# A transformer block on one Trainium2 core: fewer wait instructions, and a semaphore of its own for the gate matmuls

## The chip, the cores and the metric

The kernel runs on one core of a Trainium2 chip. A core has TensorE (PE in the profile: matmuls; PEld: the weight loads that go with them), VectorE (DVE), ScalarE (ACT), GpSimd (POOL) and SyncE (SP), which issues most DMAs here. The engines run side by side, each in its own order, and wait for each other through semaphores. The metric is the device time of one execution in microseconds; lower is better.

## The reference

```python
def _A_ref(x, wqkv, wo):                      # x: 1 x 2048 x 448, 16 heads of 28
    qkv = (x @ wqkv) split in q, k, v by head
    phi = lambda t: jnp.where(t > 0, t + 1, jnp.exp(t)) + 1e-6
    pq, pk = phi(q), phi(k)
    kv = jnp.einsum("bhsd,bhse->bhde", pk, v)
    z = jnp.einsum("bhsd->bhd", pk)
    num = jnp.einsum("bhqd,bhde->bhqe", pq, kv)
    den = jnp.einsum("bhqd,bhd->bhq", pq, z)[..., None] + 1e-6
    return (num / den, heads joined) @ wo

def _B_ref(x, w_gate, w_up, w_down):          # 448 -> 1792 -> 448
    g = jnp.einsum("bsd,df->bsf", x, w_gate)
    u = jnp.einsum("bsd,df->bsf", x, w_up)
    return jnp.einsum("bsf,fd->bsd", _gelu(g) * u, w_down)

h = x + _A_ref(_layernorm(x), wqkv, wo)
h2 = h + _B_ref(_layernorm(h), w_gate, w_up, w_down)
```

All inputs are bf16. A layer norm and linear attention are followed by a second layer norm and a gated GELU network; both have a residual.

## The kernel before

The 2048 rows are cut into 16 tiles of 128. Stage A normalizes each tile (VectorE statistics, L359 and L360; ScalarE for the reciprocal root, L366 and L368; the normalizing itself on VectorE for tiles 0 to 3, L381, and on GpSimd for the rest, L399), transposes it (tiles 0 to 3 on TensorE, L389, the rest by DMA transposes on SyncE's queue, L401), makes q and k (L415), phi (L426 to L428), and adds up the product of k and the normalized rows (L434). From that come a small key-value matrix (L473) and a folded output matrix (L493). Then, in pairs of tiles (`a2_pair`), q is divided by its denominator: a product with `zbc` (L515, L531, mostly on GpSimd), a sum (L518, L532), a reciprocal, a product (L522, L536). It is transposed, multiplied with the folded matrix (L563, L573, L574), added to the residual (L579), normalized again (L591, L608), and transposed by DMA into `hnT` (L611; the first two tiles on TensorE).

Stage B works on chunks of 2, 2, 4, 4 and 4 tiles (`B1_CHUNKS`). For each, `gu_chunk` runs over the 1792 columns of the inner width, 128 at a time. One step of it, a gate/up task, is named `gu2_v` or `gu4_v`, with v from 0 to 55 in the order of the program text: 7 pairs of matmuls with 512 columns for four tiles, 14 pairs with 256 columns for two. A pair is a gate matmul on the upper 64 rows of the array (L672) and an up matmul on the lower 64 rows (L674), issued gate first; they can run at the same time. Gate and up results have two PSUM banks each, taken in turn, so task v+2 needs the banks of task v. ScalarE makes the GELU of the gate bank in two halves of 256 columns (`ge0_v`, `ge1_v`, L692) into one of three `gl` buffers. VectorE multiplies each half with the up bank into `hh` (`hm0_v`, `hm1_v`, L694). The GELUs release the gate bank, the products the up bank. When all of `hh` for a pair of tiles is there, the down matmuls (`b2_pair`, L642; for the last two tiles `b2_tile`, L624) and the final residual additions (L648, L628) follow, and SyncE writes the result out.

Nothing is scheduled when the kernel is built. Each operation is a task with a number, and the lists in `ORDERS` fix each engine's order of tasks by number, written out by hand; parts of stage B and of stage A are interleaved in them.

Waits are made in `emit`. A task knows the tasks that it depends on (`deps`, with a place `dep_at` inside the task for those whose matmuls wait at different points, `mw=True`). Each engine has one semaphore that counts its finished tasks; each loading DMA has its own. For each dependency `emit` calls `wait_ge` unless this engine has itself waited for as much before (`waited`); what the engine knows only through another engine's waits isn't taken into account. Among the waits of one place that with the higher count goes first:

```python
for d in sorted(t.deps, key=lambda d: (t.dep_at[d.idx] if t.mw else 0, -d.ticket)):
    if waited.get(d.sem.num, 0) < d.ticket:
```

An instruction holds one wait. In the built program it is the first of a place that stays in the instruction; the others become separate wait instructions on the engine's sequencer, one or two waits each, ahead of it. In the profile they are the EVENT_SEMAPHORE records with line L164, and have no busy time. A matmul's wait shows at its weight load. A gate/up task adds one to TensorE's count with its last instruction, the last up matmul.

## Time and profile before

| | |
|---|---|
| median of 3 runs | 195.69 us (195.64 to 196.22) |
| the profiled execution | 195.62 us, of which 193.9 from its first to its last instruction |
| granted TensorE clock | 1.00 of full speed |

Busy microseconds of the engines by stretch of the span, with the number of instructions left out:

| stretch, us | what runs | TensorE | VectorE | ScalarE | GpSimd |
|---|---|---|---|---|---|
| 0 to 13 | loads, first tiles of stage A | 11.35 | 8.40 | 8.20 | 6.41 |
| 13 to 33 | q, k and their product | 20.00 | 18.63 | 12.29 | 10.70 |
| 33 to 53 | small matrices, first pairs of `a2_pair` | 18.43 | 18.95 | 16.32 | 6.67 |
| 53 to 87 | stage B for tiles 0 to 3, more of `a2_pair` | 33.83 | 30.39 | 12.12 | 16.00 |
| 87 to 120 | stage B for tiles 4 to 7, the last of `a2_pair` | 32.76 | 23.46 | 10.42 | 7.22 |
| 120 to 180 | stage B for tiles 8 to 15 | 59.81 | 27.56 | 16.46 | 5.26 |
| 180 to 193.9 | last down matmuls, output | 11.45 | 3.98 | 1.21 | 0.00 |

How to read the lines that follow below: in the timeline a row is the start in microseconds from the first instruction, the length, engine, line, operation, output and inputs, shapes, and a count of merged instructions; brackets hold the engine's idle time before it and what ended that. "64*128 64x512" is a matmul on 64 rows of the array and 128 columns of it, with 512 moving columns. A matmul's end is modelled, and neighbours overlap in the records, so TensorE counts as busy even where it stands for a moment; the distance between two starts tells more. The chain of waits lists start, length and what worked, followed back from the end; "issue" is time for which the profile shows no wait, ACTq is ScalarE's sequencer. The view of waits gives an engine, what it was about to do and what it waited for: total us, times, longest. The view of one line gives an instruction's count and its shortest, median and longest duration in ns.

### The profile page before, as it was taken

The page shows a single profiled execution, that of the slowest core. Times are in us where ns is not written, and L with a number is a line of the kernel's source. Part 1 is how long each engine was busy: PE and PEld are TensorE (multiplying, and loading weights), DVE is VectorE, ACT ScalarE, POOL GpSimd, SP SyncE. Part 2 cuts the span into 40 slices and gives each one's busy share as a digit, 9 for nine tenths or more (in the row PEclk, how much of TensorE's full clock was granted, in tenths as well). Part 3 has the DMA queues.
Part 4 walks back from the last instruction along what each step waited for, and adds up shares of the span by engine and source line. Part 5 has one row for each costly group of instructions (what it writes and reads, how often), then busy time and mean ns, then how long its engine had stood idle before and what let it go on. Part 6 is the DMA issues. An engine that isn't in the chain of part 4 may idle for free.

```text
span 193.9 us, 4577 instructions
## 1 busy us (share of the span) xinstructions
PE 187.6 (97%) x1813; PEld 109.6 (57%) x1813; DVE 131.4 (68%) x326; ACT 77.0 (40%) x220; POOL 52.3 (27%) x93
## 2 busy tenths in 40 slices
PE   7999999989999999999999999999999999999994
PEld 7545445445588768775544347756444454555643
DVE  2799987999999976998857773528435524515232
ACT  3798743878974212323224331321441424211200
POOL 8067740740228284040019400002800000000000
PEclk9999999999999999999999999999999999999999
DMA  5973558995295503761200391000092100000035
GB/s 193 374 196 64 104 110 184 218 218 110 72 266 150 95 3 49 98 116 29 47 3 0 76 138 28 0 3 25 1 142 49 51 0 0 3 0 0 3 132 178
DMA packets 34597, 17.12 MB, mean 88 GB/s; under 512 B 26832, under 2 KB 33168, under 8 KB 34576
## 3 DMA queue, kind: packets, MB, share of 16 engines
q1 hardware_dynamic: 34432, 16.72, 39.3%
q8 instruction: 14, 0.23, 0.5%
q10 hardware_dynamic: 144, 0.11, 0.3%
q14 instruction: 7, 0.06, 0.1%
HBM read 8.26 MB, written 1.84 MB: 52 GB/s over the span
## 4 chain that ended last, share of the span: by engine, by line
PE 83%; DVE 10%; ACT 3%; issue 2%; DMA 1%; ACTq 0%; DVEq 0%
PE ps L674 29%; PE ps L642 18%; PE ps L672 12%; PE ps L415 9%; PE ps L434 5%; PE ps L624 3%; PE ps L573 3%; DVE hh L694 2%; PE ps L574 2%; ACT gl L692 1%; DMA x_sb<-in_A_x_dram 1%; DVE den L518 1%; DVE pqn L522 1%; DVE st L359 1%; DVE eq L528 1%
## 5 line engine op out<-in xcount | busy, mean ns | idle before, releaser
L674 PE MATMUL ps<-hnT,wgu_sb 64*128 64x512 bf16 (+1 forms) x490 | 89.8, 334 | 0.4
L672 PE MATMUL ps<-hnT,wgu_sb 64*128 64x512 bf16 (+1 forms) x490 | 89.8, 333 | 0.0
L692 ACT ACTIVATE gl<-ps 128x256 bf16<-128x256 f32 x112 | 36.8, 382 | 85.6 <-PE ps L674 73.6
L694 DVE TENSOR_TENSOR hh<-ps,gl 128x256 bf16<-128x256 f32 x112 | 43.2, 417 | 40.5 <-ACT gl L692 40.3
L674 PEld LDWEIGHTS ps<-hnT,wgu_sb 64*128 64x128 bf16 x490 | 44.4, 94 | 31.0 <-DVE hh L694 6.9
L672 PEld LDWEIGHTS ps<-hnT,wgu_sb 64*128 64x128 bf16 x490 | 44.8, 94 | 6.5 <-DVE hnT L606 0.2
L642 PE MATMUL ps<-wd_sb,hh 64*128 64x448 bf16 x392 | 41.7, 349 | 0.2 <-DVE hh L694 0.2
L642 PEld LDWEIGHTS ps<-wd_sb,hh 64*128 64x128 bf16 x392 | 23.4, 94 | 14.9 <-DVE hh L694 1.6
L415 PE MATMUL ps<-wqk_sb,xnT 128*128 128x448 bf16 x128 | 27.4, 352 | 0.0
L359 DVE BATCH_NORM_STATS2 st<-x_sb 128x6 f32<-128x448 bf16 x32 | 19.1, 614 | 3.7 <-DMA x_sb<-in_A_x_dram 3.5
L415 PEld LDWEIGHTS ps<-wqk_sb,xnT 128*128 128x128 bf16 x128 | 12.1, 98 | 11.3 <-DVE pk L428 0.5
L531 POOL TENSOR_TENSOR t<-pq,zbc 128x448 f32<-128x448 bf16 x12 | 12.6, 1067 | 16.5 <-DVE pq L529 16.5
L434 PE MATMUL ps<-pk,xnn 128*128 128x448 bf16 x64 | 14.3, 353 | 0.0
L648 DVE TENSOR_TENSOR x_sb<-ps,x_sb 128x448 bf16<-128x448 f32 x14 | 8.4, 618 | 7.7 <-PE ps L642 7.7
L573 PE MATMUL ps<-w,pqnT 64*128 64x448 bf16 x49 | 11.5, 349 | 0.1
L363 POOL TENSOR_SCALAR nm<-mv 128x1 f32<-128x1 f32 (+1 forms) x19 | 4.1, 228 | 26.6 <-DVE mv L360 26.3
L426 ACT ACTIVATE e<-ps 128x448 bf16<-128x448 f32 x16 | 8.6, 540 | 5.6 <-PE ps L415 3.0
L399 POOL TENSOR_SCALAR xnn<-x_sb,nm,rs 128x448 bf16<-128x448 bf16 x12 | 9.6, 804 | 3.5 <-ACT rs L368 3.1
L608 POOL TENSOR_SCALAR hn<-x_sb,nm,rs 128x448 bf16<-128x448 bf16 x14 | 10.3, 745 | 0.5
L574 PE MATMUL ps<-pt_sb,pqnT 64*128 64x448 bf16 x42 | 10.2, 350 | 0.0
L371 POOL TENSOR_SCALAR ln<-mv 128x2 f32<-128x2 f32 x7 | 1.5, 222 | 32.1 <-DVE mv L360 31.9
L579 DVE TENSOR_TENSOR x_sb<-ps,x_sb 128x448 bf16<-128x448 f32 x16 | 9.7, 615 | 0.7 <-PE ps L574 0.6
(83 smaller groups left out, 166.9 us busy)
## 6 DMA issues: line engine op xcount, KB each, us to landing
out_dram<-x_sb SPq DMA_DIRECT2D x15, 112.0 KB, 1.8
wd_sb<-in_B_w_down_dram SPq DMA_DIRECT2D x1, 1568.0 KB, 7.5
x_sb<-in_A_x_dram SPq DMA_DIRECT2D x3, 448.0 KB, 5.6
wgu_sb<-in_B_w_gate_dram SPq DMA_DIRECT2D x1, 896.0 KB, 12.8
wgu_sb<-in_B_w_up_dram SPq DMA_DIRECT2D x1, 896.0 KB, 15.8
wqk_sb<-in_A_wqkv_dram SPq DMA_DIRECT2D x1, 672.0 KB, 4.5
wgu_sb<-in_B_w_gate_dram SPq DMA_DIRECT2D x1, 672.0 KB, 5.8
wgu_sb<-in_B_w_up_dram SPq DMA_DIRECT2D x1, 672.0 KB, 8.3
```

Source lines behind the costliest of these rows:

```text
L359: op("dve", lambda e: e.bn_stats(st[:, t, :], src_ap), [b_src], [b_st[t]], "bnst%s_%d" % (tag, t))
L415: ins = e.matmul(ps[:, bk, 0:D], xnT[:, t, k, :], wqk_sb[:, k, c0:c0 + D], start=(k == 0), stop=(k == 3))
L434: ins = e.matmul(ps[:, BK_PT[c], 0:D], xnn[:, t % XN_R, c * 128:(c + 1) * 128], pk[:, ip, :], start=(t == 0), stop=(t == T - 1))
L531: op("pool", lambda e, n=n: e.tensor_tensor(t1[:, n, :], pq[:, a + n, :], zbc[:, :], ALU.mult), [b_pq[a + n]] + b_z, [b_t1[n]], "t1p_%d" % ...
L573: e.matmul(ps[:, BK_OUT[0], 0:D], pqnT[ra, i2, sg // 2, :], w2[ra, sg // 2, :], start=(sg == 0), stop=(sg == 5))
L574: ins = e.matmul(ps[:, BK_OUT[1], 0:D], pqnT[rb, i2, 3 + (sg + 1) // 2, :], (w2 if sg == 6 else w2s)[rb, sg // 2, :], start=(sg == 0), sto ...
L608: op("pool", lambda e, t=t, sh=sh: e.tensor_scalar(hn[:, sh, 0:D], x_sb[:, t, :], nm2[:, t:t + 1], rs2[:, t:t + 1], ALU.add, ALU.mult), [b ...
L642: ins = e.matmul(ps[:, BK_O[n], 0:D], hh[rows, j, sl[n]], wd_sb[rows, j, :], start=(half == 0 and j == 0), stop=(half == 1 and j == NJ - 1))
L672: e.matmul(psG[:, jj * N:(jj + 1) * N], wgu_sb[A_, k, j * 128:(j + 1) * 128], hnT[A_, ka_, c0:c0 + N], start=(k == 0), stop=(k == NK - 1))
L674: ins = e.matmul(psU[:, jj * N:(jj + 1) * N], wgu_sb[B_, k, j * 128:(j + 1) * 128], hnT[B_, kb_, c0:c0 + N], start=(k == 0), stop=(k == NK ...
L692: G.add("act", lambda e, gi=gi, cs_=cs_, psG=psG: e.activation(gl[:, gi, cs_], psG[:, cs_], AF.Gelu_apprx_tanh), r=[b_ps[BK_G[i]]], w=[b_g ...
L694: op("dve", lambda e, dst=dst, srcU=srcU, srcL=srcL: e.tensor_tensor(dst, srcU, srcL, ALU.mult), [b_ps[BK_U[i]], b_glh], [b_ar[j_][t % HR] ...
```

## The change

`plan` replaces the part of `emit` that picked the waits. It walks over the tasks in an order in which each comes after what it depends on, and keeps for each engine what it knows of every semaphore: what it waited for, and what the tasks it waited for knew in their turn. A wait that this implies is dropped, also against the other waits of the same task. Where two or more waits remain in one place, a table `HOLD` names, for 14 tasks, the dependency whose wait goes first and so stays in the instruction; elsewhere the higher count still goes first.

A gate/up task is now told which of its outputs is finished early (`half`, the gate bank). Its last gate matmul adds one to a new semaphore `pe_mark`, and a task that only reads the gate bank (the GELUs) waits for that instead of TensorE's count. The products in `hh` and everything else that depends on the task wait for its end as before. The orders are the same, and so is every other instruction.

In the built programs the separate wait instructions go from 69 to 8 on ScalarE, from 42 to 29 on TensorE, from 71 to 51 on VectorE, from 27 to 15 on GpSimd and from 20 to 2 on SyncE (some of these stand in the program's start and end and not at L164). TensorE's instructions that add to a semaphore go from 152 to 208.

```diff
+HOLD = {
+    30: (29,), 35: (32,), 71: (61,), 173: (172,), 186: (185,), 247: (246,), 292: (290,), 321: (300,), 360: (304,),
+    496: (376,), 546: (545,), 779: (670,), 827: (824,), 835: (834,),
+}
...
-    def add(self, eng, fn, r=(), w=(), name="", kind="op", after=(), mw=False, cost=(), sync=()):
+    def add(self, eng, fn, r=(), w=(), name="", kind="op", after=(), mw=False, cost=(), sync=(), half=()):
...
+        t.half, t.early, t.full, t.nearly, t.mark = list(half), set(), set(), 0, None
...
         for b, k in r:
             dep(b.writer, k)
+            (t.early if b in b.writer.half else t.full).add(b.writer.idx)
         for b, k in w:
-            dep(b.writer, k)
-            for rd in b.readers:
-                dep(rd, k)
+            for d in [b.writer] + b.readers:
+                if d is not None:
+                    dep(d, k)
+                    t.full.add(d.idx)
+        t.early -= t.full
+        for d in t.deps:
+            if d.idx in t.early:
+                d.nearly += 1
...
+                if t.nearly:
+                    nmark += 1
+                    t.mark = (mark_sem, nmark)
+        self.plan()
+
+    def signal(self, t, d):
+        return d.mark if d.idx in t.early else (d.sem, d.ticket)
+
+    def plan(self):
+        now, after, self.waits = {e: {} for e in ENGS}, {}, {}
+        for t in self.topo:
+            k0 = now[t.eng]
+            want = []
+            for d in t.deps:
+                sem, n = self.signal(t, d)
+                want.append([sem, n, t.dep_at[d.idx] if t.mw else 0, after[d.idx][d.idx in t.early], d.idx])
+            want = [w for w in want if k0.get(w[0].num, 0) < w[1]]
+            keep = [w for w in want if not any(
+                v is not w and v[2] <= w[2] and (v[3].get(w[0].num, 0) >= w[1] if v[0].num != w[0].num else (v[1] > w[1] or v[1] == w[1] and v[2] < w[2]))
+                for v in want)]
+            k1 = dict(k0)
+            for sem, n, slot, know, idx in keep:
+                for a, b in know.items():
+                    k1[a] = max(k1.get(a, 0), b)
+                k1[sem.num] = max(k1.get(sem.num, 0), n)
+            now[t.eng] = k1
...
+            hold = HOLD.get(t.idx, ())
+            slots = {}
+            for w in sorted(keep, key=lambda w: (w[4] not in hold, -w[1])):
+                slots.setdefault(w[2], []).append((w[0], w[1], w[4]))
+            self.waits[t.idx] = slots
 
     def emit(self, ename, eng):
-        waited = {}
         for t in self.order[ename]:
-            slots = {}
-            for d in sorted(t.deps, key=lambda d: (t.dep_at[d.idx] if t.mw else 0, -d.ticket)):
-                if waited.get(d.sem.num, 0) < d.ticket:
-                    waited[d.sem.num] = d.ticket
-                    slots.setdefault(t.dep_at[d.idx] if t.mw else 0, []).append((d.sem, d.ticket))
+            slots = dict(self.waits[t.idx])
...
+            if t.half:
+                ins, first = ins
+                if t.mark:
+                    first.then_inc(t.mark[0], 1)
...
-                            e.matmul(psG[:, jj * N:(jj + 1) * N], wgu_sb[A_, k, j * 128:(j + 1) * 128], hnT[A_, ka_, c0:c0 + N], start=(k == 0), stop=(k == NK - 1))
+                            first = e.matmul(psG[:, jj * N:(jj + 1) * N], wgu_sb[A_, k, j * 128:(j + 1) * 128], hnT[A_, ka_, c0:c0 + N], start=(k == 0), stop=(k == NK - 1))
...
-                    return ins
-                G.add("pe", fngu, ..., name="gu%d_%d" % (nt, v), mw=True)
+                    return ins, first
+                G.add("pe", fngu, ..., name="gu%d_%d" % (nt, v), mw=True, half=[b_ps[BK_G[i]]])
```

More of the change, by code (lines that the diff above doesn't have):

```diff
@@ L61 @@
 class _Task:
-    __slots__ = ("eng", "fn", "deps", "name", "ticket", "sem", "ncons", "kind", "idx", "after", "dep_at", "mw", "cost")
+    __slots__ = ("eng", "fn", "deps", "name", "ticket", "sem", "ncons", "kind", "idx", "after", "dep_at", "mw", "cost", "half", "early", "full", "nearly", "mark")
 class _Graph:
@@ L120, in place @@
         assert sorted(t.idx for o in self.order.values() for t in o) == list(range(len(self.all)))
[L121 removed]
+        done, at, self.topo = set(), {e: 0 for e in ENGS}, []
         while len(done) < len(self.all):
@@ L151, in finalize @@
                     t.ticket = cnt[e]
+                if t.nearly:
[22 more added lines that the diff above has]
+            now[t.eng] = k1
+            e1 = dict(k1) if t.ticket is not None or t.mark else k1
+            e0 = dict(k0)
+            if t.mark:
+                e0[t.mark[0].num] = e1[t.mark[0].num] = t.mark[1]
+            if t.ticket is not None:
+                e1[t.sem.num] = max(e1.get(t.sem.num, 0), t.ticket)
+            after[t.idx] = (e1, e0)
+            hold = HOLD.get(t.idx, ())
[3 more added lines that the diff above has]
+            self.waits[t.idx] = slots
@@ L170, in emit @@
                 ins = t.fn(eng)
+            if t.half:
+                ins, first = ins
+                if t.mark:
+                    first.then_inc(t.mark[0], 1)
             if t.kind in ("dma", "dma_out"):
```

9 lines of the change are left out of this document (5 added, 4 removed).

## The prediction

> **What bounds the kernel now.** I read the page first (busy shares, then the chain that ended last), then the waits between engines, then the chain and the timeline around single stalls.
>
> ```profile
> span 193.9 us, 4577 instructions
> PE 187.6 (97%) x1813; PEld 109.6 (57%) x1813; DVE 131.4 (68%) x326; ACT 77.0 (40%) x220; POOL 52.3 (27%) x93
> PE 83%; DVE 10%; ACT 3%; issue 2%; DMA 1%; ACTq 0%; DVEq 0%
> ...
> PEld ps L674 <- DVE hh L694: 6.9, 18, 0.6
> ```
>
> TensorE is busy for 97% of the span and carries 83% of the chain, so only three things can shorten the run: the start, the stretch from 33 to 53 us where VectorE works without a gap, and the short stops of TensorE behind VectorE's product `hh` (L694) in the second half. Eighteen waits of 6.9 us look like much, but that is the weight load's idle time, and most of it lies under matmuls that are still running. What a stop costs is read from the distance of the gate matmuls (L672):
>
> ```profile
> 79.98 0.27 PE L672 MATMUL ps<-hnT,wgu_sb 64*128 64x256 bf16 x1
> 80.21 0.28 PE L672 MATMUL ps<-hnT,wgu_sb 64*128 64x256 bf16 x1
> ...
> 85.92 0.35 PE L642 MATMUL ps<-wd_sb,hh 64*128 64x448 bf16 x1
> 86.44 0.69 PE L642 MATMUL ps<-wd_sb,hh 64*128 64x448 bf16 x4 [0.17 <-DVE hh L694]
> ...
> 100.77 0.38 PE L672 MATMUL ps<-hnT,wgu_sb 64*128 64x512 bf16 x1
> 101.09 0.39 PE L672 MATMUL ps<-hnT,wgu_sb 64*128 64x512 bf16 x1
> ...
> 108.79 0.38 PE L672 MATMUL ps<-hnT,wgu_sb 64*128 64x512 bf16 x1
> 109.01 0.38 PE L672 MATMUL ps<-hnT,wgu_sb 64*128 64x512 bf16 x1
> 109.52 0.39 PE L672 MATMUL ps<-hnT,wgu_sb 64*128 64x512 bf16 x1
> ...
> 112.34 0.38 PE L672 MATMUL ps<-hnT,wgu_sb 64*128 64x512 bf16 x1
> 112.83 0.39 PE L672 MATMUL ps<-hnT,wgu_sb 64*128 64x512 bf16 x1
> ...
> 125.80 0.38 PE L672 MATMUL ps<-hnT,wgu_sb 64*128 64x512 bf16 x1
> 126.14 0.39 PE L672 MATMUL ps<-hnT,wgu_sb 64*128 64x512 bf16 x1
> ...
> 137.45 0.38 PE L672 MATMUL ps<-hnT,wgu_sb 64*128 64x512 bf16 x1
> 137.94 0.39 PE L672 MATMUL ps<-hnT,wgu_sb 64*128 64x512 bf16 x1
> ...
> 140.75 0.38 PE L672 MATMUL ps<-hnT,wgu_sb 64*128 64x512 bf16 x1
> 141.13 0.39 PE L672 MATMUL ps<-hnT,wgu_sb 64*128 64x512 bf16 x1
> ...
> 152.65 0.38 PE L672 MATMUL ps<-hnT,wgu_sb 64*128 64x512 bf16 x1
> 153.11 0.39 PE L672 MATMUL ps<-hnT,wgu_sb 64*128 64x512 bf16 x1
> ```
>
> Undisturbed, gate matmuls of 512 columns follow each other by 0.22 us (108.79 to 109.01) and those of 256 by half of it; that is one slot. What exceeds a slot is lost: 0.12 us at 79.98, 0.10 at 100.77, 0.29 at 109.01, 0.27 at 112.34, 0.12 at 125.80, 0.27 at 137.45, 0.16 at 140.75 and 0.24 at 152.65, together 1.57. At 85.92 a down matmul (448 columns, so 0.19 a slot) is 0.52 from the next: another 0.33.
>
> Each is the same loop, here that of 109.01 in the chain of waits (start, length):
>
> ```profile
> 107.66 0.23 PE ps L674
> ...
> 107.91 0.02 ACTq L164
> 107.97 0.72 ACT gl L692 x2
> ...
> 108.71 0.77 DVE hh L694 x2
> 109.52 0.39 PE ps L674
> ```
>
> The up matmul of a chunk ends at 107.88, ScalarE spends 0.10 on a separate wait instruction (L164) before its two GELUs start, VectorE follows with two products, and only then is the PSUM bank free for the next chunk but one. Whatever the GELUs start earlier, the bank comes free earlier.
>
> **The change part by part.** The order of the work is the same on all engines in the two built programs; only wait instructions and one semaphore differ.
>
> *The gate's own mark.* The row group of the gate can run one slot ahead of that of the up matmuls. The last chunk shows it, because no gate matmul follows there:
>
> ```profile
> 179.91 0.38 PE L672 MATMUL ps<-hnT,wgu_sb 64*128 64x512 bf16 x1
> ...
> 180.12 0.38 PE L674 MATMUL ps<-hnT,wgu_sb 64*128 64x512 bf16 x1
> ...
> 180.54 0.66 ACT L692 ACTIVATE gl<-ps 128x256 bf16<-128x256 f32 x2 [5.01 <-PE ps L674]
> ```
>
> The last gate matmul starts at 179.91, the last up matmul at 180.12. Today the GELU starts at 180.54, 0.04 after the up matmul's end (180.12 + 0.38 = 180.50); released by the gate it could start 0.21 earlier. This is also the hop of a GELU whose only wait sits in the instruction: 0.04, against 0.10 (107.88 to 107.97) with a separate wait instruction. So a release gains 0.06 from the wait and, from the lead, between 0 (both groups in step) and 0.21. The lead arises when an up matmul is held for a busy bank while the gate matmul before it runs on; it stays until the gate's group has to wait. I take it as nothing at 79.98, where nothing was held before; as half a slot at 85.92 (0.05 to 0.06) and about two thirds at 109.01, because the stops that made it shrink themselves; and as full after that. The VectorE product still waits for the whole chunk. That is covered: its two GELUs take 0.72 us and the up matmul's end comes at most 0.21 after the gate's.
>
> Gains per stop, never more than the stop itself: 0.06 at 79.98; 0.14 at 85.92 (0.06 plus half a slot there, and what is gained upstream moves with it); 0.10 at 100.77 (all); 0.20 of 0.29 at 109.01; 0.27 at 112.34, 0.12 at 125.80, 0.27 at 137.45, 0.16 at 140.75 and 0.24 at 152.65 (all). Sum 1.56.
>
> The added work is one increment on the last gate matmul of each of 56 chunks (490 gate matmuls, 7 or 14 a chunk). The last up matmul of each chunk has always carried one; one lies between 108.79 and 109.01, and that distance is the usual slot. So I take 0 and keep 0.01 each, the resolution of the rows, as the upper end: 0 to 0.56. A rule of the Trainium skill speaks against the change here: "TensorE: Matmul & The Clock Gate", section "The cost: per-tile semaphore tail", has increments serialize at 26.3 ns each. That would be an estimated 1.47 us for 56; the rows show no such step after the up matmul's increment, which is why it is a rival below and not a term of the sum.
>
> *Implied waits dropped.* What is cut are these separate waits:
>
> ```profile
> L164 ACTq EVENT_SEMAPHORE  x67: 17/38/38, 4.4 to 180.6; - x67
> ```
>
> Of ScalarE's 67 the built program keeps 6. TensorE's, VectorE's, GpSimd's and SyncE's fall too. Where an engine is busy or the wait long over, this gains nothing: TensorE's removed waits stand in stretches without a stop, and most of VectorE's stand before L428, where it works without a gap. They count where an engine idles for the last of two waits. That is so at the start:
>
> ```profile
> 8.89 0.20 ACT L368 ACTIVATE rs<-ln 128x1 f32<-128x1 f32 x1
> ...
> 9.20 0.40 DVE L381 TENSOR_SCALAR xnn<-x_sb,mv,rs 128x448 bf16<-128x448 bf16 x1 [0.39 <-ACT rs L368]
> ```
>
> From ScalarE's end at 9.09 to the start at 9.20 are 0.11; with one wait, as above, 0.04. The gain of 0.07 reaches TensorE, which waits for this row; a second hop of the kind, normalize to transpose of tile 0, now keeps the expected last wait in the matmul and gives about 0.06. I take 0.13 (0 to 0.2). The last addition (L628) loses its separate wait on the path to the end: 0.07 by the same difference. The stretch from 33 to 53 us I leave at 0 (up to 0.1): no instruction on VectorE's chain there changes its wait.
>
> *The new wait.* The gain meets one transfer:
>
> ```profile
> 108.22 5.30 SPq L611 DMA_TRANSPOSE hnT<-hn  x4
> ...
> 116.92 0.37 PE L672 MATMUL ps<-hnT,wgu_sb 64*128 64x512 bf16 x1
> 116.99 0.38 PE L674 MATMUL ps<-hnT,wgu_sb 64*128 64x512 bf16 x1
> ```
>
> At 116.92 the gate's lead is down to 0.07: the chunk already waited some 0.14 for the last of four transposes of `hnT`. By then TensorE has gained 0.13 + 0.06 + 0.14 + 0.10 + 0.20 + 0.27 = 0.90. The transposes go back to a GELU before 108.22, so they get what was gained up to 100.77 (0.13 + 0.06 + 0.14 + 0.10 = 0.43), that GELU's own 0.06 plus about 0.14 of lead, and 0.12 within the 5.30 us, where SyncE no longer runs three wait instructions between them (an estimate, 0.04 each, from the hops above): 0.75. So 0.15 is given back (0 if GpSimd's and VectorE's earlier finish brings them further forward, 0.47 if they get no more than the 0.43).
>
> The sum: 1.56 + 0.13 + 0.07 − 0.15 = 1.61 us less. The profiled execution took 195.62 us (span 193.9, 1.7 around it), 0.07 under the median of 195.69. 195.62 − 1.61 = **194.0**. By its own bounds (0 to 0.47 given back, increments up to 0.56, a third more or less of the lead) it runs from 193.3 to 194.8.
>
> **The rivals.** *The mark brings no lead:* if the gate's increment becomes visible no earlier than the chunk's end, only 0.06 is left at each of the nine places. 0.54 + 0.13 + 0.07 = 0.74, the transposes cost nothing more: 194.9. For it: the ends of matmuls are modelled, and no release by a gate is in this trace. Against: the start times 179.91 and 180.12 are a slot apart.
>
> *Increments cost:* 0.56 by the rows' bound on top of the forecast, 194.6; if they stand in series on the path, as the page cited has it, an estimated 195.5.
>
> *The transfers hold it back twice:* `hnT` is also refilled for the last chunks. If at 116.92 only the 0.43 come through and the next group is as late, 0.47 is lost twice instead of 0.15 once: 0.79 more, 194.8.
>
> *Slower: VectorE shut out by GpSimd.*
>
> ```profile
> 36.00 2.04 POOL L515 TENSOR_TENSOR t<-pq,zbc 128x448 f32<-128x448 bf16 x2
> ...
> 36.66 1.63 DVE L528 TENSOR_SCALAR eq<-eq 128x896 bf16<-128x896 bf16 x1
> ...
> 49.06 0.36 DVE L528 TENSOR_SCALAR eq<-eq 128x896 bf16<-128x896 bf16 x1
> ```
>
> The same operation takes 0.36 us alone and 1.63 under GpSimd's two products, ending just after them. GpSimd loses waits before these products, so they start up to 0.06 earlier, and one that gets in ahead of a VectorE operation which now goes first stops it for about a product's length, 1.02 us. From 33 to 53 us VectorE has no slack, so this goes straight into the time. Two such turns eat the forecast, three give 194.0 + 3.06 = 197.1. Against it: the starts move by 0.06 only, and an operation already shut out ends earlier when the product does. The Trainium skill ("SBUF — State Buffer", section "Who interferes with whom") has the shared ports as a lock that whoever issues first keeps for its whole instruction; by that rule, as by the rows, only a change of who comes first costs anything.
>
> **How the numbers follow.** Forecast 0.56 (193.3 to 194.8 is its own range); a still larger gain, should the stop at 85.92 and the transposes both dissolve, 0.05; no lead 0.16; increments 0.05; transfers 0.09; GpSimd 0.09. The range 193.2 to 195.4 leaves out some 0.04 below and, above, GpSimd and the dearer part of the increments, about 0.12. A change under 0.3% (0.59 us, so 195.1 to 196.3) can't be told from none here. Faster: 0.56 + 0.05 + 0.09 + 0.11 of the no-lead case + 0.02 of the increments = 0.83. Same: 0.05 + 0.03 + 0.03 of GpSimd (two turns) = 0.11. Slower: the other 0.06 of GpSimd.
>
> **What would show it.** After the change ScalarE should have some 6 separate wait instructions; a GELU should start 0.04 after the last gate matmul's end and, in chunks with a lead, before the up matmul ends. The gate rows that answer to 112.34, 137.45 and 152.65 should be 0.22 to 0.25 apart; if they stay 0.4 apart, the mark brings no lead. Undisturbed gate rows stay 0.22 apart; 0.23 or more across a chunk's end shows that increments cost. The wait for `hnT` at the first chunk after 115 us should be 0.2 to 0.4 and not larger. L528's first row stays near 1.6 us; more long rows beside it would show the slower rival. A time over 195.4 would make the prediction wrong, and so would a faster one in which those gate rows haven't moved.

## The result, and the profile after

| | before | after |
|---|---|---|
| median, first measurement (4 runs each) | 195.94 us | 193.93 us (193.65 to 194.29), ratio 0.9899 (0.9872 to 0.9926) |
| the same kernels in a second measurement | 195.63 us | 193.99 us (193.46 to 194.80), ratio 0.9920 (0.9896 to 0.9945) |
| the profiled execution | 195.62 us, span 193.9 | 194.29 us, span 192.5 |

The change makes the kernel about 1% faster; the forecast was 194.0. The profiled execution after is the slowest of its four, so the trace shows only 1.33 of the 1.6 to 2.0 us. The page after, first lines, chain and the weight loads of the up matmuls:

```profile
span 192.5 us, 4453 instructions
PE 185.7 (96%) x1813; PEld 115.3 (60%) x1813; DVE 131.5 (68%) x326; ACT 77.0 (40%) x220; POOL 52.4 (27%) x93
...
PE 83%; DVE 8%; DMA 4%; POOL 1%; issue 1%; ACT 1%; SPq 0%; POOLq 0%
...
L724 PEld LDWEIGHTS ps<-hnT,wgu_sb 64*128 64x128 bf16 x490 | 45.1, 94 | 26.2 <-DVE hh L744 2.7
```

The wait for VectorE's products (L694 of before is L744 now) fell from 6.9 to 2.7 us. The share of transfers in the chain rose from 1% to 4%: a new wait, below. The view of the line that makes the waits (L210 now) shows 6 of ScalarE's 67 left, 49 of VectorE's 69:

```profile
L210 DVEq EVENT_SEMAPHORE  x49: 21/21/21, 55.2 to 177.7; - x49
...
L210 ACTq EVENT_SEMAPHORE  x6: 17/17/17, 1.3 to 168.8; - x6
```

The last chunk shows the release (timeline; L722 gate, L724 up, L742 GELU):

```profile
178.55 0.38 PE L722 MATMUL ps<-hnT,wgu_sb 64*128 64x512 bf16 x1
...
178.76 0.38 PE L724 MATMUL ps<-hnT,wgu_sb 64*128 64x512 bf16 x1
...
178.97 0.66 ACT L742 ACTIVATE gl<-ps 128x256 bf16<-128x256 f32 x2 [5.01 <-PE ps L722]
```

The last gate matmul ends at 178.55 + 0.38 = 178.93, the GELU starts 0.04 later, and the up matmul runs until 179.14. The rows that answer to 112.34, 137.45 and 152.65 have no stop any more; the first two rows of each chunk, and the rows after the place where `hnT` was late at 116.92:

```profile
112.28 0.38 PE L722 MATMUL ps<-hnT,wgu_sb 64*128 64x512 bf16 x1
...
112.50 0.38 PE L722 MATMUL ps<-hnT,wgu_sb 64*128 64x512 bf16 x1
...
116.44 0.38 PE L722 MATMUL ps<-hnT,wgu_sb 64*128 64x512 bf16 x1
...
116.64 0.38 PE L724 MATMUL ps<-hnT,wgu_sb 64*128 64x512 bf16 x1
...
136.82 0.38 PE L722 MATMUL ps<-hnT,wgu_sb 64*128 64x512 bf16 x1
...
137.04 0.38 PE L722 MATMUL ps<-hnT,wgu_sb 64*128 64x512 bf16 x1
...
151.56 0.38 PE L722 MATMUL ps<-hnT,wgu_sb 64*128 64x512 bf16 x1
...
151.77 0.38 PE L722 MATMUL ps<-hnT,wgu_sb 64*128 64x512 bf16 x1
```

They stand 0.21 to 0.22 apart, against 0.49, 0.49 and 0.46 before, and at 116.44 the gate is a whole slot (0.20) ahead of the up matmul. The new wait stands at 19.49, in TensorE's rows of q and k (L465):

```profile
19.49 0.92 PE L465 MATMUL ps<-wqk_sb,xnT 128*128 128x448 bf16 x4
21.31 0.55 PE L465 MATMUL ps<-wqk_sb,xnT 128*128 128x448 bf16 x2 [0.90 <-DMA xnT<-xnn]
```

Four matmuls of 448 columns take 0.75 us, so the next four were due at 20.24 and came 1.07 late: the k of tile 7 waits for the transpose of its `xnT`. Before, all eight ran in one row:

```profile
19.87 1.68 PE L415 MATMUL ps<-wqk_sb,xnT 128*128 128x448 bf16 x8
```

Where the time went is read best from five places of TensorE's order, by the starts of their rows: the k of tile 9 (19.87 before), the output matmuls at 51.30, the down matmuls at 83.73, the chunk at 116.92 and the last pair of down matmuls at 180.13.

| from one place to the next, us | before | after | gain | predicted |
|---|---|---|---|---|
| start to k of tile 9 | 19.87 | 19.49 | 0.38 | 0.13 |
| to the output matmuls | 31.43 | 32.33 | −0.90 | 0 |
| to the down matmuls (stop at 79.98) | 32.43 | 32.24 | 0.19 | 0.06 |
| to the chunk at 116.92 (stops at 85.92 to 112.34, `hnT`) | 33.19 | 32.38 | 0.81 | 0.71 − 0.15 |
| to the last down pair (stops at 125.80 to 152.65) | 63.21 | 62.33 | 0.88 | 0.79 |
| to the end of the span | 13.77 | 13.73 | 0.04 | 0.07 |

Stage B gave 1.88 us instead of 1.41; the stretch from 19 to 51 us, which was to stay as it is, took back 0.90.

### The profile page after: what moved, and what is told of

It reads as the page before. It is cut to its first block, busy times and chain, and to the rows that moved or that the text cites. A ratio compares the mean times of both kernels' runs of the same rounds, so it can differ in the third digit from the quotient of the medians.

```text
span 192.5 us, 4453 instructions
## 1 busy us (share of the span) xinstructions
PE 185.7 (96%) x1813; PEld 115.3 (60%) x1813; DVE 131.5 (68%) x326; ACT 77.0 (40%) x220; POOL 52.4 (27%) x93
## 4 chain that ended last, share of the span: by engine, by line
PE 83%; DVE 8%; DMA 4%; POOL 1%; issue 1%; ACT 1%; SPq 0%; POOLq 0%
PE ps L724 32%; PE ps L692 18%; PE ps L722 13%; PE ps L465 8%; PE ps L484 4%; PE ps L674 3%; PE ps L623 3%; DMA x_sb<-in_A_x_dram 2%; DMA xnT<-xnn 2%; PE ps L624 2%; DVE st L409 1%; DVE den L568 1%; DVE pqn L572 1%; DVE eq L578 1%; PE ps L613 1%
## 5 line engine op out<-in xcount | busy, mean ns | idle before, releaser
L724 PE MATMUL ps<-hnT,wgu_sb 64*128 64x512 bf16 (+1 forms) x490 | 88.7, 333 | 0.0
L722 PE MATMUL ps<-hnT,wgu_sb 64*128 64x512 bf16 (+1 forms) x490 | 88.6, 333 | 0.0
L742 ACT ACTIVATE gl<-ps 128x256 bf16<-128x256 f32 x112 | 36.8, 382 | 83.2 <-PE ps L722 83.2
L744 DVE TENSOR_TENSOR hh<-ps,gl 128x256 bf16<-128x256 f32 x112 | 43.1, 416 | 37.0 <-ACT gl L742 36.8
L724 PEld LDWEIGHTS ps<-hnT,wgu_sb 64*128 64x128 bf16 x490 | 45.1, 94 | 26.2 <-DVE hh L744 2.7
L722 PEld LDWEIGHTS ps<-hnT,wgu_sb 64*128 64x128 bf16 x490 | 45.5, 94 | 5.0 <-DVE hnT L656 0.2
L692 PEld LDWEIGHTS ps<-wd_sb,hh 64*128 64x128 bf16 x392 | 24.3, 94 | 13.7 <-DVE hh L744 1.3
L465 PE MATMUL ps<-wqk_sb,xnT 128*128 128x448 bf16 x128 | 27.5, 353 | 0.9 <-DMA xnT<-xnn 0.9
L409 DVE BATCH_NORM_STATS2 st<-x_sb 128x6 f32<-128x448 bf16 x32 | 19.1, 614 | 3.8 <-DMA x_sb<-in_A_x_dram 3.7
L465 PEld LDWEIGHTS ps<-wqk_sb,xnT 128*128 128x128 bf16 x128 | 12.1, 98 | 12.3 <-DMA xnT<-xnn 1.3
L484 PE MATMUL ps<-pk,xnn 128*128 128x448 bf16 x64 | 14.2, 352 | 0.0
L658 POOL TENSOR_SCALAR hn<-x_sb,nm,rs 128x448 bf16<-128x448 bf16 x14 | 10.4, 751 | 0.5
## 6 DMA issues: line engine op xcount, KB each, us to landing
wgu_sb<-in_B_w_up_dram SPq DMA_DIRECT2D x1, 896.0 KB, 15.7
```

Of the source, the lines that this page charges most:

```text
L409: op("dve", lambda e: e.bn_stats(st[:, t, :], src_ap), [b_src], [b_st[t]], "bnst%s_%d" % (tag, t))
L465: ins = e.matmul(ps[:, bk, 0:D], xnT[:, t, k, :], wqk_sb[:, k, c0:c0 + D], start=(k == 0), stop=(k == 3))
L484: ins = e.matmul(ps[:, BK_PT[c], 0:D], xnn[:, t % XN_R, c * 128:(c + 1) * 128], pk[:, ip, :], start=(t == 0), stop=(t == T - 1))
L658: op("pool", lambda e, t=t, sh=sh: e.tensor_scalar(hn[:, sh, 0:D], x_sb[:, t, :], nm2[:, t:t + 1], rs2[:, t:t + 1], ALU.add, ALU.mult), [b ...
L692: ins = e.matmul(ps[:, BK_O[n], 0:D], hh[rows, j, sl[n]], wd_sb[rows, j, :], start=(half == 0 and j == 0), stop=(half == 1 and j == NJ - 1))
L722: first = e.matmul(psG[:, jj * N:(jj + 1) * N], wgu_sb[A_, k, j * 128:(j + 1) * 128], hnT[A_, ka_, c0:c0 + N], start=(k == 0), stop=(k == ...
```

## The experiments

Each kernel was timed in five rounds beside the kernel before on the same chip. Ratios are to that kernel, with their 95% interval; the changed kernel has 0.990 and 0.992.

| run | median, us | ratio (interval) |
|---|---|---|
| without the mark | 195.45 | 0.998 (0.997 to 1.000) |
| the mark alone | 194.34 | 0.994 (0.992 to 0.995) |
| no held waits | 194.04 | 0.992 (0.990 to 0.993) |
| 434 more increments | 194.06 | 0.992 (0.990 to 0.994) |
| ScalarE's program as long as before | 194.13 | 0.993 (0.991 to 0.995) |
| four programs as long as before | 194.62 | 0.995 (0.993 to 0.997) |
| ScalarE's program moved | 194.36 | 0.993 (0.991 to 0.995) |
| three programs moved | 196.46 | 1.005 (1.002 to 1.007) |
| GpSimd's program moved | 194.02 | 0.992 (0.990 to 0.994) |
| order on VectorE | 193.95 | 0.991 (0.990 to 0.993) |
| order, and two programs moved | 193.57 | 0.988 (0.986 to 0.990) |

The changed kernel itself ran again beside two of them (GpSimd's program moved, order on VectorE); its second time above is from there:

> The changed kernel itself, as a measure for the two beside it: 193.9 us, ratio to before 0.990 to 0.992, executions spread from 193.6 to 194.3 with the length of the wait for the transpose of xnT at 19.5 us (0.3 to 1.1).

Line numbers in the rows of these kernels differ by up to three from those of the changed one.

**Without the mark.**

```diff
-            (t.early if b in b.writer.half else t.full).add(b.writer.idx)
+            t.full.add(b.writer.idx)
```

> The implied waits stay dropped and the held waits stay held; the GELUs wait for the whole chunk again. Theory (the gate matmul's lead is what removes the stops): of the nine stops only the 0.06 us of the separate wait instruction is gained, 0.54 instead of the 1.57 found in the changed kernel's gate rows, so about 193.9 + 1.0 = 194.9 us, with the gate rows that answer to 112.34 and 137.45 still 0.4 us apart and GELUs 0.04 after the up matmul. Rival (the dropped wait instructions alone remove the stops): 193.9 us, rows 0.22 apart.

Measured: 195.45 us. The stops are back, in TensorE's timeline:

```profile
111.83 0.38 PE L722 MATMUL ps<-hnT,wgu_sb 64*128 64x512 bf16 x1
...
112.23 0.39 PE L722 MATMUL ps<-hnT,wgu_sb 64*128 64x512 bf16 x1
```

0.40 apart, as the theory had it, where the kernel before has 0.49 and the changed one 0.22. The rival falls. The 0.5 us above the expected 194.9 come mostly from the chunk after the down matmuls, which waits for `hnT`: from 83.40 to it are 33.38 us, against 32.38 with the mark. Of that 1.00 us, 0.34 are the stops at 109.01 and 112.34 (their rows are 0.38 and 0.40 apart, a slot being 0.22); the rest, 0.66, is the wait. What is known of it is in the part on why the prediction was right.

**The mark alone.**

```diff
             keep = [w for w in want if not any(
-                v is not w and v[2] <= w[2] and (v[3].get(w[0].num, 0) >= w[1] if v[0].num != w[0].num else (v[1] > w[1] or v[1] == w[1] and v[2] < w[2]))
+                v is not w and v[2] <= w[2] and v[0].num == w[0].num and (v[1] > w[1] or v[1] == w[1] and v[2] < w[2])
                 for v in want)]
...
-                for a, b in know.items():
-                    k1[a] = max(k1.get(a, 0), b)
...
-            hold = HOLD.get(t.idx, ())
+            hold = ()
```

> The mark stays; waits are picked as before the change (no implied wait dropped, none held). GELUs then start about 0.10 us after the last gate matmul's end instead of 0.04, the start loses 0.13 and the end 0.07, and some 0.3 us of the stops comes back: 0.5 us more than the changed kernel. Theory (the new 1.07 us wait of the q and k matmuls for a transpose of xnT at 19.5 us comes from an instruction fetch that moved because engines run fewer instructions): the wait is gone, under 0.2 us, since the instructions are those of before, and the time is about 193.9 + 0.5 - 1.0 = 193.4 us. Rival (it comes from the earlier start, TensorE running into the transposes): most of the start's gain is gone too, but the wait shrinks only by the 0.2 us by which the start moves back, and the time is about 194.3 us.

Measured: 194.34 us. In the gate rows (L720 here) the mark takes 0.49 to 0.28; the last 0.06 are what the prediction gave for the separate wait instruction:

```profile
111.73 0.38 PE L720 MATMUL ps<-hnT,wgu_sb 64*128 64x512 bf16 x1
...
112.01 0.39 PE L720 MATMUL ps<-hnT,wgu_sb 64*128 64x512 bf16 x1
```

The wait at 19.5 us is gone as the theory expected (31.46 us from the k of tile 9 to the output matmuls, 31.43 before), but the time is the rival's. Two sizes were off: stage B lost 0.63 and not 0.3 against the changed kernel (32.41 + 32.64 + 62.53 against 32.24 + 32.38 + 62.33), and the profiled execution of the changed kernel, with its 1.07 of wait, is the slowest of its four, so the others will have waited less. So the mark alone is worth about 1.2 us, the dropped waits alone 0.1, both 1.6 to 2.0. That the dropped waits show so little by themselves has two reasons in the trace of the run without the mark: the new wait at 19.5 us (0.37 there) and the late `hnT` (0.66).

**No held waits.**

```diff
-            hold = HOLD.get(t.idx, ())
+            hold = ()
```

> As the changed kernel, but where two waits remain the higher count stays in the instruction everywhere. Theory (the held wait is worth one hop of 0.06 us, and only the one on the start's path counts): 0.06 to 0.1 us more, 194.0 us. Rival (the held waits carry much of the gain): 0.5 us more or above, 194.4 us.

Measured: 194.04 us beside 193.93 and 193.99. What `HOLD` brings, if anything, is under what the intervals can tell; a large part in the gain is excluded.

**More increments.**

```diff
+                            if first is not None:
+                                first.then_inc(G.spare, 1)
                             first = e.matmul(psG[:, jj * N:(jj + 1) * N], ...)
```

> As the changed kernel, and each of the other 434 gate matmuls also adds one to a semaphore that nobody waits for. Theory (an increment costs TensorE nothing, as in the gate rows): 193.9 us, gate rows 0.22 us apart. Rival (increments stand in series at a price each): at the 0.01 us that the rows could hide, 4.3 us more, 198.2 us; by the 26.3 ns each of the Trainium skill (TensorE: Matmul & The Clock Gate, The cost: per-tile semaphore tail) an estimated 11.4 us more, 205.3 us.

Measured: 194.06 us, by the medians 0.1 more than the changed kernel for 434 increments. The gate rows (L725 here):

```profile
112.08 0.38 PE L725 MATMUL ps<-hnT,wgu_sb 64*128 64x512 bf16 x1
...
112.29 0.38 PE L725 MATMUL ps<-hnT,wgu_sb 64*128 64x512 bf16 x1
```

0.21 apart, with an increment on each. The price is 0.3 ns for one by the medians (0.13 us by 434), and 2 ns by the far ends of the intervals (0.9943 and 0.9896 of 195.6 us, 0.9 us). The Trainium skill's 26.3 ns ("TensorE: Matmul & The Clock Gate", "The cost: per-tile semaphore tail") does not show in matmuls of this length.

**What makes the transpose late: length of the programs.** In the view of transfers, the changed kernel fetches 8 KB of instructions in a window of 0.1 us from 19.5 (first row below: queue, packets, MB, share of the window); the transpose for tile 7 was issued at 17.7 and landed 3.6 us later (view of the tile `xnT`, SyncE's instructions; the durations are those of the issue):

```profile
q14 instruction: 1, 0.01, 24.1%
```
```profile
L451 SPq DMA_TRANSPOSE xnT<-xnn x1: 1265/1265/1265, 17.7 to 17.7; - x1
...
DMA to landing us min/median/max: 3.6/3.6/3.6
```

In the kernel before, no fetch lies between 17.9 and 21 us, and the same transpose lands after 2.5:

```profile
L401 SPq DMA_TRANSPOSE xnT<-xnn x1: 1264/1264/1264, 18.0 to 18.0; - x1
...
DMA to landing us min/median/max: 2.5/2.5/2.5
```

All kernels up to here whose implied waits were dropped have a fetch at 19.1 to 19.6 us and the wait, of 0.28 to 1.07 us; both kernels with the old waits have no fetch there, the first one at 21.3 to 21.6, and no wait. The first guess was that the place of a fetch depends on the length of the program.

```diff
+        for i in range({'act': 122}.get(ename, 0)):
+            eng.wait_ge(self.sems["dve"], i // 2 + 1)
         if ename == "sp":
```

(this is the run with ScalarE's program padded; the other has `{'act': 122, 'dve': 40, 'pool': 24, 'sp': 36}`)

> As the changed kernel, with 61 wait instructions, all long fulfilled, appended at the end of ScalarE's program, where ScalarE is idle; its program is then as long as before the change. Every instruction ahead of the end is that of the changed kernel. Theory (the wait for the transpose of xnT at 19.5 us is an 8 KB instruction fetch, ScalarE's, that lands among the transposes, and the place of the fetch depends on the length of the program): the fetch at 19.1 to 19.6 us goes back to about 26.5 us, TensorE waits under 0.1 us there instead of 0.3 to 1.1 (mean of the four kernels with the dropped waits: 0.66), and the time is 193.9 - 0.6 = 193.3 us. Rival (the earlier start alone makes TensorE run into the transposes, or the fetch belongs to another engine or a fixed place in the stream): fetch and wait stay, 193.9 to 194.0 us.

> As the run with the longer ScalarE program, and VectorE's, GpSimd's and SyncE's programs are padded in the same way at their ends to their lengths of before (20, 12 and 18 instructions). Theory: the 8 KB fetches fall as before the change, near 21.4, 26.6, 41.9, 76, 109, 134 and 188 us, no wait for xnT is left, 193.3 us; if a fetch of another engine than ScalarE's is the one at 19.1 to 19.6 us, this run shows it where the other doesn't. Rival (length of the programs has no say): 193.9 to 194.0 us with the fetch near 19.5 us.

Measured: 194.13 and 194.62 us, with the fetch at 19.0 and 19.4. The length has no say; this theory fell. The run with four padded programs had a slower end besides (14.2 us from the last down pair, not 13.7), with an instruction fetch at 191.8 us. In its profiled execution the transpose had been issued 0.55 us earlier and the fetch found only the next one, which had time to spare: no wait.

**What makes the transpose late: place of the fetch.** Long fulfilled waits at the front of a program move everything behind them.

```diff
         for t in self.order[ename]:
+            for i in range({30: 48}.get(t.idx, 0)):
+                eng.wait_ge(self.sems["pool"], 1 + i % 2)
```

(two waits make one instruction; task 30 is ScalarE's first activation; with three programs `{30: 48, 97: 68, 28: 80}`, with GpSimd's `{97: 68}`)

> As the changed kernel, with 24 wait instructions, all long fulfilled, put ahead of ScalarE's first activation, where it idles from 2.5 to 4.4 us; so each later instruction of ScalarE stands 24 places further back in its program. Theory (an 8 KB instruction fetch in flight together with a transpose makes that transpose 0.7 to 1.1 us late; the fetch at 19.0 to 19.6 us is ScalarE's and comes at a fixed place of its program): that fetch moves to about 11 us, where the transposes have 1.5 us to spare, the transpose that tile 7's k waits for lands 2.5 us after its issue and not 3.2 to 3.6, and TensorE's wait there falls from 0.3 to 1.1 us to under 0.1. Some of it comes back at the next two fetches (22 and 24.8 us), 0.1 and 0.4: 193.6 us. Rival (it isn't ScalarE's fetch, or fetches have nothing to do with the late transposes): fetch, wait and time stay, 193.9 to 194.1 us.

> The same on three engines: 24 such instructions ahead of ScalarE's first activation, 34 ahead of GpSimd's first operation after the fills of the start, 40 ahead of VectorE's first (all three idle there). Theory: the fetches at 19.5, 22 and 24.8 us move to about 10 to 12 us, all transposes of xnT from 17 us on land 2.5 us after their issue, no wait for them is left, and the time is 193.9 - 0.66 = 193.3 us, unless a later fetch falls on the transposes of hnT. Rival (late transposes are not the fetches' doing): latencies over 3 us and the wait stay, 193.9 to 194.1 us.

> As the changed kernel, with 34 wait instructions, all long fulfilled, ahead of GpSimd's first operation after the fills of the start. Theory (the instruction fetch at 19.0 to 19.6 us is GpSimd's, since it stayed when ScalarE's program was moved and went when all three were): that fetch moves to about 11 to 13 us, where the transposes have 1.5 us to spare; the transpose for tile 7 lands 2.5 us after its issue, and TensorE's wait for it is under 0.1 instead of 0.3 to 1.1. The fetches at 22 and 24.6 us stay and give some 0.2 of it back: 193.9 - 0.66 + 0.2 = 193.4 us. Rival (SyncE's fetch, or none of them): fetch, wait and time stay, 193.9 us.

Measured: 194.36, 196.46 and 194.02 us. With ScalarE's program moved, the fetch at 22 us went to 11.8 and that at 19.3 stayed, so ScalarE's was the wrong one to name; but the transpose issued at 20.0, which took 3.2 us in the changed kernel, takes 2.5 now. The median of 194.36 is not explained by that: the trace is of the fastest of the six executions (193.81). The view of `xnT`, first the changed kernel, then this one:

```profile
L451 SPq DMA_TRANSPOSE xnT<-xnn x1: 1264/1264/1264, 20.3 to 20.3; - x1
...
DMA to landing us min/median/max: 3.2/3.2/3.2
```
```profile
L454 SPq DMA_TRANSPOSE xnT<-xnn x1: 1264/1264/1264, 20.0 to 20.0; - x1
...
DMA to landing us min/median/max: 2.5/2.5/2.5
```

With GpSimd's program moved, the fetch at 24.8 went to 15.7, the transpose issued at 22.9 fell from 3.2 to 2.5, and the fetch found another transpose instead, that of tile 6, on which TensorE now waits (in the changed kernel it takes 3.45 us, with a 16 KB fetch at 14.6 that is here as well):

```profile
L454 SPq DMA_TRANSPOSE xnT<-xnn x1: 2470/2470/2470, 13.8 to 13.8; - x1
...
DMA to landing us min/median/max: 4.3/4.3/4.3
```
```profile
18.22 0.93 PE L468 MATMUL ps<-wqk_sb,xnT 128*128 128x448 bf16 x4 [0.26 <-DMA xnT<-xnn]
```

That is the mechanism by itself: the fetch moved, and the lateness and a stop moved with it. With three programs moved, the 8 KB fetches lie at 10.4, 14.9 and 18.8 us and every transpose issued from 19.4 on lands within 2.6 us of its issue; the time is spoilt by my own padding, since one such wait costs VectorE's sequencer 0.098 us ((4.8 − 1.1) / 38 in its row), so its first operation starts at 5.0 and not 3.5. That is 1.5 of the 3.3 us by which the k of tile 9 comes later (22.81 and 19.49); the rest is not taken apart. The waits of this run:

```profile
L208 DVEq EVENT_SEMAPHORE  x39: 50/50/50, 1.1 to 4.8; - x39
L208 POOLq EVENT_SEMAPHORE  x33: 42/43/43, 1.1 to 3.9; - x33
L208 ACTq EVENT_SEMAPHORE  x23: 17/38/38, 1.2 to 2.9; - x23
```

**The stop at 85.92 that did not shrink.** After the change it stands at 86.81. VectorE's rows, after:

```profile
83.90 1.99 DVE L586 TENSOR_TENSOR pqn<-pq,rd 128x896 bf16<-128x896 bf16 x1
85.81 0.61 DVE L629 TENSOR_TENSOR x_sb<-ps,x_sb 128x448 bf16<-128x448 f32 x1
86.34 0.74 DVE L744 TENSOR_TENSOR hh<-ps,gl 128x256 bf16<-128x256 f32 x2
```

The product `hh` that TensorE waits for stands behind `pqn`, which runs beside GpSimd's two products (82.89 to 84.93 in the timeline), and behind an addition. The GELU had ended at 84.92 (84.26 + 0.66): its release has nothing to do with this stop. Before the change it was the same: the GELU ended at 84.78, `pqn` ran from 83.76 to 85.51, and the addition and the product came behind it.

```diff
-544 481 528 530 649
+481 528 530 544 649
```

(cut from a longer line of numbers, VectorE's order: 544 is `pqn`, 481 and 528/530 the addition and the products)

> As the changed kernel, but on VectorE the product with the reciprocals (pqn, 1.99 us long beside GpSimd's two products of 2.04 us) goes behind the residual addition and the two products hh that TensorE waits for at 86.8 us. Theory (the stop in the down matmuls that the change left is VectorE's queue behind pqn, which GpSimd shuts out, not the release of a GELU): pqn alone takes about 1.1 us and ends near 86.4, the stop of 0.35 us above the change of row groups vanishes, 193.9 - 0.35 = 193.6 us. Rival (what VectorE does here has a cover elsewhere: the transposes of pqn or hnT come later and TensorE waits there): 0.35 us gained at 87 us and given back by 115 us, 193.9 us; more given back than gained, above 194.2 us.

VectorE's rows with the new order, and TensorE's at the place of the stop:

```profile
84.67 0.76 DVE L744 TENSOR_TENSOR hh<-ps,gl 128x256 bf16<-128x256 f32 x2 [0.60 <-ACT gl L742]
85.34 1.08 DVE L586 TENSOR_TENSOR pqn<-pq,rd 128x896 bf16<-128x896 bf16 x1
```
```profile
83.78 2.84 PE L692 MATMUL ps<-wd_sb,hh 64*128 64x448 bf16 x28
86.43 0.38 PE L722 MATMUL ps<-hnT,wgu_sb 64*128 64x512 bf16 x1
```

All 28 down matmuls run without a gap, in 2.65 us instead of 3.29, and `pqn` takes 1.08 us instead of 1.99. The Trainium skill ("SBUF — State Buffer", "Who interferes with whom") has issue order decide which of VectorE and GpSimd blocks. The rows agree as far as they go: with the old order, GpSimd's two products ran from 82.89 to 84.93, `pqn` was issued among them at 83.90 and ended 0.96 us after them (85.89); with the new order it starts 0.68 after GpSimd's products have ended (84.66). No row here has it issued first with a product beside it. In the profiled execution, the fastest of its six, 31.90 us are left of the 32.38 from the down matmuls to the chunk at 116 us. Yet the median is 193.95, no better than without the new order. In the profiled execution nothing of the gain is given back (62.33 and 13.72 us follow); that the others lose it is the rival's cover, likely but seen only in the run of the next part. `pqn` now ends 0.5 us later, 0.8 counted from the first down matmul, and its transpose, with a 16 KB fetch beside it at 86.8, is the last thing that the next output matmuls need. Here TensorE stood 0.13 us for it (89.24 to 89.59 between two starts, less a slot); in the run of the next part it stood longer.

**Both, with VectorE's program moved in place of GpSimd's.**

```diff
+            for i in range({30: 48, 28: 46}.get(t.idx, 0)):
+                eng.wait_ge(self.sems["pool"], 1 + i % 2)
...
-544 481 528 530 649
+481 528 530 544 649
```

> The changed kernel with the order of VectorE from the run before (pqn behind the products that TensorE waits for), 24 long fulfilled wait instructions ahead of ScalarE's first activation, and 22 ahead of VectorE's first operation, which end before its first data land at 3.5 us (they took 0.098 us each on VectorE in the run with three padded engines). Theory (the fetch at 19.0 to 19.6 us is VectorE's: it stayed when ScalarE's and when GpSimd's program was moved, and was gone when VectorE's was moved too): it moves to 11 to 14 us, ScalarE's to 12 us, the transpose for tile 7 lands 2.5 us after its issue, TensorE's wait for it (0.3 to 1.1 us in all kernels with the dropped waits but one) is under 0.1, some 0.3 us comes back for tile 11 behind GpSimd's fetch at 24.8 us, and the stop at 86.8 us stays away: 193.95 - 0.6 + 0.2 = 193.5 us or less. Rival (the earlier fetches only choose another transpose, that of tile 6, and TensorE waits there): a wait of 0.4 us at 17 us, 193.9 us.

Measured: 193.57 us (193.00 to 193.78), ratio 0.988 (0.986 to 0.990): about 0.4 us under the changed kernel, which is at the edge of what the intervals separate. Two fetches lie at 12.0 us, the transpose for tile 7 lands after 2.5 us, and the wait is gone: the eight matmuls of tiles 9 and 7 are one row.

```profile
19.85 1.68 PE L468 MATMUL ps<-wqk_sb,xnT 128*128 128x448 bf16 x8
```

So the fetch at 19.5 us was VectorE's: it stayed at 19.3 with ScalarE's program moved alone and at 19.5 with the new order alone. In this profiled execution, the slowest of its six, the gain of the new order was lost again, to the transpose of `pqn` (the first row is from the chain of waits, the second from TensorE's timeline, where L626 is an output matmul):

```profile
86.09 3.75 DMA pqnT<-pqn
```
```profile
89.89 0.36 PE L626 MATMUL ps<-w,pqnT 64*128 64x448 bf16 x1 [0.61 <-DMA pqnT<-pqn]
```

## Why the prediction was right, and where not

The time was right to 0.1 us, and the mechanism with the most weight is shown. That it was so close is luck in part. Against the kernel before, the gain was 2.0 us in the first measurement and 1.6 in the second, for 1.61 in the sum; and in the profiled execution two misses of opposite sign meet: stage B and the start gave 0.72 us more than forecast (0.47 and 0.25), and the stretch from 19 to 51 us lost 0.90 that no term had.

- **The mark** does what it was to do. Without it 1.5 us are lost, of which 0.66 are the late `hnT`; alone it brings 1.2. GELUs start 0.04 after the last gate matmul and ahead of the up matmul's end. "The mark brings no lead" is out. The lead was sized too small at 109.01: that stop vanished whole (rows 0.22 apart, 0.38 without the mark).
- **The stop at 79.98** vanished too, with 0.19 in the stretch to the down matmuls instead of 0.06, but not by the mark: without it the gate rows there are 0.11 apart and the stretch is 32.24 us, with the mark alone they are 0.23 apart and it is 32.41 (32.43 before). So this stop was not "the same loop" either. Its GELU had ended at 78.64 (77.98 + 0.66), its products started at 79.22 and 79.74, and VectorE worked up to them without a gap, from a copy on that ran beside GpSimd's normalizing. Before and after:

```profile
77.28 0.72 POOL L608 TENSOR_SCALAR hn<-x_sb,nm,rs 128x448 bf16<-128x448 bf16 x1
77.52 0.61 DVE L610 COPY hn<-hn 128x448 bf16<-128x448 bf16 x1
```
```profile
77.82 0.81 POOL L658 TENSOR_SCALAR hn<-x_sb,nm,rs 128x448 bf16<-128x448 bf16 x1
77.91 0.30 DVE L660 COPY hn<-hn 128x448 bf16<-128x448 bf16 x1
```

  The copy took 0.61 and 0.62 us in the two kernels with the old waits and 0.29 to 0.30 in the others, where it comes sooner after GpSimd's start. It is the turn that the prediction feared as its slower rival, in the other direction. Which dropped wait brought it about is not shown.
- **Increments** cost nothing that can be measured (434 of them, 0.13 us by the medians), so that rival is out.
- **The stop at 85.92**, of which 0.14 was to go, stayed. The step that failed put it in "the same loop" of GELU and product. The chain shown for 109.01 was not the chain there: VectorE's `pqn` under GpSimd's product was, and a new order on VectorE removed it.
- **The 0.15 given back at 116.92** did not come; the chunk's own wait of some 0.14 went as well (its gate is 0.20 ahead of the up matmul now, 0.07 before). The step took the lateness of `hnT` for the length of SyncE's chain (5.30 us). It was one transpose, landing 4.5 us after its issue at 112.2, where the three before it took 3.1 to 3.2. After the change it goes out at 111.8 and lands after 3.0; it took 4.8 without the mark and 4.7 with the mark alone, and in these two runs as in the kernel before the chunk starts 0.20 after the landing. Why it was late is open. A 16 KB instruction fetch lies beside it in all three, but the changed kernel has the same fetch at the same distance from the issue as the run without the mark (2.4 us, at 114.2 in both) and is not late. So this part of the gain is luck: no step foresaw it. The view of `hnT` before (two transposes, so the longest is the one) and after:

```profile
L611 SPq DMA_TRANSPOSE hnT<-hn x2: 1249/1270/1290, 110.9 to 112.2; - x2
...
DMA to landing us min/median/max: 3.1/3.8/4.5
```
```profile
L661 SPq DMA_TRANSPOSE hnT<-hn x2: 1299/1301/1303, 110.4 to 111.8; - x2
...
DMA to landing us min/median/max: 3.0/3.1/3.1
```

- **33 to 53 us at 0** held; but the new wait stands ahead of it, at 19.5 us, and no step priced it. I had asked which instructions drop out and what each was worth, not what else moves when a program loses instructions: the fetches of the program itself. It costs 0.3 to 1.1 us; without it the profiled execution would have gained an estimated 2.2 us (1.33 + 0.90).
- **The start**: 0.38 gained where 0.13 was said, but other kernels with the same start reach the k of tile 9 between 19.37 and 19.88, so this term can't be told from the spread of the first loads. **The end**: 0.04 against 0.07.
- **Transfers holding it back twice**: not at 116.92. In the group of `hnT` behind it, TensorE waited in two runs: without held waits (62.73 us up to the last down pair instead of 62.33) and, by 0.10, with ScalarE's program moved.
- **GpSimd shutting VectorE out more often** did not happen: VectorE is busy for 131.5 us, 131.4 before, and the one turn that was found (the copy at 77.52) went in its favour.

What stays open: why there is a fetch at 19.1 to 19.6 us once waits are dropped. The length of the program is excluded, and the moved programs support a place that goes with the instructions ahead of it. But by that rule fewer instructions ahead should bring a fetch later, and the first one came earlier (21.6 to 19.6 us); whose fetch the one at 21.6 is was not found. Open too is what makes the transpose of `hnT` at 112 us late in some kernels.

## What to carry to other kernels

A consumer that needs only half of a task's output should be released by the last instruction that makes it; where two row groups of TensorE share the work, that was worth up to a slot for each stop here, and the increments cost nothing that could be measured. Where two engines run beside each other with little between their starts, a few dropped waits can change which comes first. Before a stop is put down to one chain because its neighbours have that chain, read the chain at the stop itself. And where instructions are added or removed while transposes run with a few tenths of slack, look for the instruction fetches in the view of transfers before and after: they move with the program, and so does the transpose that they make late.

## What the runs showed of the hardware

- A DMA transpose of one tile into `xnT` takes 2.4 to 2.6 us from issue to landing with no instruction fetch beside it, one into `hnT` 2.9 to 3.2. What an 8 KB fetch does to one into `xnT` goes by when it begins: 1.2 to 2.1 us after the issue, the transpose took 3.2 to 3.6 us (2.7 in one case); under 0.8 or over 2.2 us after it, 2.4 to 2.7, and 0.9 to 1.0 us after it, 2.5 to 3.0. For `hnT` no such rule came out: 16 KB fetches 2.4 to 2.8 us after the issue went with 3.0 us in some executions and 4.3 to 5.1 in others.
- A copy of VectorE from and to SBUF (448 columns, bf16) took 0.61 us when issued 0.24 us into an operation of GpSimd, and 0.30 when issued 0.09 after its start, where GpSimd's operation took 0.81 instead of 0.72.
- A wait instruction of its own that is long fulfilled costs the sequencer 0.098 us on VectorE, about 0.08 on ScalarE ((2.9 − 1.2) / 22) and 0.09 on GpSimd ((3.9 − 1.1) / 32), though its record shows 0.050, 0.038 and 0.043.
- From the output matmuls at 51 us on, up to the last pair of down matmuls, executions of different kernels with the same order repeat to 0.01 us (32.24, 32.38 and 62.33 us by the five places, in the changed kernel's two profiled executions and in five of the variants). What differs between these lies ahead, in the loads and the transposes, but for the slower end of the run with four padded programs.
